# A new opening for the first chunk of a fused attention and expert kernel: row sums by one-column matmuls, the feature map on ScalarE and GpSimd, halves of heads instead of halves of the batch, and other load times

## The chip, the core and the metric

The kernel runs on one core of a Trainium2 chip. A core has TensorE (matmuls and transposes), VectorE, ScalarE and GpSimd for the rest, and SyncE, which here issues nearly all transfers. Each engine works through its own queue in order. The metric is the device time of one execution in microseconds (us). Times inside an execution are counted from its first instruction.

## The reference, cut to what matters

Two batches, eight heads, 576 positions, 64 wide. Attention output is a gated mix of causal softmax attention and of a lookup in a memory matrix through the feature map phi; two feed-forward layers follow.

```python
scores = np.where(causal, -1e9, scale * (q @ k.T))
a = np.exp(scores - scores.max(-1, keepdims=True))
a /= a.sum(-1, keepdims=True) + 1e-09
local = a @ v
phi = lambda x: np.where(x > 0, x, np.exp(x) - 1.0) + 1.0
mem_out = (phi(q) @ M_prev) / ((phi(q) @ z_prev)[..., None] + 1e-06)
x = sigmoid(beta) * mem_out + (1 - sigmoid(beta)) * local   # then to (B*S, H*D)
x = np.maximum(x @ w_in, 0.0) ** 2 @ w_out                  # 512 -> 2048 -> 512
out = sum(p[e] * (np.maximum(x @ w1[e], 0.0) @ w2[e]) for e in range(4))
```

The weights `w_in` and `w_out` reach the chip as float64 words, and the kernel turns them into float32 itself.

## The kernel before, in words

Tokens are cut into nine tiles of 128, in three chunks. Chunk 0 is the first 128 rows of both batches (tiles 7 and 8). Chunk 1 holds rows 128 to 383, chunk 2 the rest. The change touches two stages: the opening, which does the attention of chunk 0, and the stage behind it, in which the first layer of chunk 0 runs on TensorE while the attention of chunk 1 is woven in.

**The opening** (`opening`, called at the end of a block in which every engine keeps the program's order). Its order is a written list of letters. `s0` and `s1` step through the scores of heads 0 to 3 and 4 to 7, each for both batches: first the matmuls (L307), then one maximum per batch (VectorE, L189 and L318), then one exponential per batch (ScalarE, L324), which also gives the row sums by its accumulator. `p0`, `p1` are the halves of the feature map (`phi`, L181 to L184): an exponential on ScalarE, then a minimum and a maximum on VectorE. `m0` to `m2` are the memory matmuls (L405), `n` and `k` their norms and products on VectorE (L410 to L417). `t0` to `t3` transpose the four blocks of exponentials (L336) and copy them out of PSUM, three on VectorE (L339) and one on ScalarE (L341). `v0` to `v3` are the products with the values (L356). `q` turns row sums into weights (L424 to L426), `x0` and `x1` weigh and add one batch each (L432, L433), and `o0`, `o1` transpose the result (L197) and copy it into the layer's input `y` (L438). `g` is the gate, `l` and `L` load the second rows. `c` is a step of the conversion, `S` a step of the first scores of chunk 1, and `w` readies the layer.

**The conversion** (`convert`): each block of 512 KB of float64 words is loaded (L722), read twice by ScalarE (`mag` L734, `bits` L737), joined twice by VectorE (L740, L745), and the float32 block is written back to memory for later chunks (L748). A block's load stands in SyncE's queue behind the write of the block made three blocks before.

**The layer of chunk 0** (`ffn1(0)`) gives one step for each of 128 matmuls of 256 columns: four up (L101) for a block of hidden units, the squared relu (ScalarE L787, VectorE L788), and four down (L802) two blocks later. If a block of weights isn't converted when the layer comes to it, the conversion's steps are put into the queues right there. Before the third up block that holds for the blocks numbered 4 and 5.

**The woven work** (`rest`) has a due step for each item: third rows are loaded (`x.load(2, n)`), the second rows' feature map (`x.phis(1)`, L181 to L184) and memory matmuls (`x.mem(1, ...)`, L365) run, and pairs of heads go through scores, turns, values and blends. A due step is rounded up to a whole step of the layer.

Of the kernel before, what the change touches and what calls it, by code (L numbers as in the profile page):

```python
# [21 lines left out]
P = 128  # L22
# [30 lines left out]
def attention_then_experts(ctx, tc, qa, ka, va, qc, kc, vc, mz, beta, w1, probs, w2, out):  # L53
# [116 lines left out]
    def gates():  # L170
# [5 lines left out]
        nc.vector.tensor_scalar(out=gate1, in0=gate, scalar1=-1.0, scalar2=1.0, op0=ALU.mult, op1=ALU.add)  # L176
        yield

    def phi(out, e, q, hold=lambda x: x):

        hold(nc.scalar.activation(out=e, in_=q, func=AF.Exp))  # L181
        yield
        nc.vector.tensor_scalar_min(e, e, 1.0)
        nc.vector.scalar_tensor_tensor(out=out, in0=q, scalar=1.0, in1=e, op0=ALU.add, op1=ALU.max)  # L184
        yield
# [44 lines left out]
    def opening(c0, c1, first_layer):  # L230

        sc = [c0.scores(p, spot) for p, spot in zip(c0.pairs, (("s", 3), ("pv", 2)))]
        ph, gt, later = c0.phis(0), gates(), c1.scores(c1.pairs[0])
        units = [u for p in c0.pairs for u in p]
        steps = dict(
            g=lambda: next(gt), c=lambda: next(cv), w=lambda: next(first_layer), l=lambda: [c1.load(1, n) for n in range(2)], L=lambda: c1.load(1, 2), S=lambda: next(later, None),
            n=c0.norms, k=c0.recall, q=c0.weights,
        )
        for i in range(2):
            steps[f"s{i}"] = lambda i=i: next(sc[i], None)  # L240
            steps[f"p{i}"] = lambda i=i: next(ph[i])
            steps[f"x{i}"] = lambda i=i: c0.local(i)
            steps[f"o{i}"] = lambda i=i: c0.out(i)
        for i, u in enumerate(units):
            steps[f"t{i}"] = lambda u=u, e=nc.vector if i < 3 else None: c0.turn(u, e)
            steps[f"v{i}"] = lambda u=u: c0.values(u)
        for i in range(3):
            steps[f"m{i}"] = lambda i=i: c0.states(i)


        order = (
            "c l c L s0 p0 p0 g g p1 s1 s0 s0 s0 s1 s1 p1 m0 t0 s1 t2 s0 s1 m1 m2 n t1 v0 v2 k q x0 "
            "t3 c v1 v3 S o0 x1 o1 c S S c w S S S"
        )
        for k in order.split():
            steps[k]()

    def attention_a(c, pool, eng, banks):
# [25 lines left out]

        def phis(r):
            e = q[r][1] = pool.tile([P, H, P], F32, tag="phia", name="phia", bufs=2)
            return [phi(e[:, hs], e[:, hs], q[r][0][:, hs]) for hs in (slice(0, 4), slice(4, 8))]

        def s_(pair, spot=None):
            scs = {}  # L290
            tag, bufs = spot or ("s", banks[1])
            for u in pair:
                t, kn, h0, nh = u
                b = TILES[t][0][0]
                if h0 + b == 0:
                    sms[t] = pool.tile([P, B, H], F32, tag="sm", name="sm", bufs=2)
                if h0 == 0:
                    st[t] = [pool.tile([P, H], F32, tag=x, name=x, bufs=4) for x in ("mx", "nb")] + [sms[t - b][:, b]]
# [45 lines left out]
        def v_(u):  # L344
            t, kn, h0, nh = u
            b = TILES[t][0][0]
            at = at_.pop(u)
# [47 lines left out]
            b = TILES[t][0][0]  # L395
            finish(t, xls[t - b][:, b], banks[0], banks[2])()

        pms, fs = [], [pool.tile([P, B, H], F32, name=f"f{i}", bufs=1) for i in range(2 * (c == 0))]
        third = (slice(0, 3), slice(3, 6), slice(6, 8))

        def states(i):
            ps, tag, bufs = (banks[0], "m", banks[2]) if i < 2 else (ps_h, "h", 1)
            pms.append(ps.tile([P, 3, B, D + 1], F32, tag=tag, name="pm", bufs=bufs))
            for k, h in enumerate(range(third[i].start, third[i].stop)):
                nc.tensor.matmul(pms[i][:, k], lhsT=q[0][1][:, h, :], rhs=mzd[:, h], start=True, stop=True)  # L405

        def norms():
            for pm, hs in zip(pms, third):
                n = hs.stop - hs.start
                nc.vector.tensor_scalar_add(fs[1][:, :, hs], pm[:, 0:n, :, D].rearrange("p h b -> p b h"), 1e-6)  # L410
            nc.vector.reciprocal(out=fs[1], in_=fs[1])
            nc.vector.tensor_mul(fs[1], fs[1], gate[:, None, :].to_broadcast([P, B, H]))

        def recall():
            for pm, hs in zip(pms, third):
                n = hs.stop - hs.start
                nc.vector.tensor_mul(  # L417
                    q[0][2][:, :, hs, 0:D].rearrange("p b h d -> p h b d"), pm[:, 0:n, :, 0:D],
                    fs[1][:, :, hs].rearrange("p b h -> p h b")[:, :, :, None].to_broadcast([P, n, B, D]),
                )  # L420

        def weights():
            for b in range(B):
                nc.vector.tensor_scalar_add(fs[0][:, b], st[CHUNKS[0][0] + b][2], 1e-9)  # L424
            nc.vector.reciprocal(out=fs[0], in_=fs[0])
            nc.vector.tensor_mul(fs[0], fs[0], gate1[:, None, :].to_broadcast([P, B, H]))  # L426

        def local(b):
            xl = xls[b] = pool.tile([P, H, D], F32, tag="xl0", name="xl0", bufs=2)
            for i in range(2):  # L430
                hs = slice(4 * i, 4 * i + 4)
                nc.vector.tensor_mul(xl[:, hs], pvs[CHUNKS[0][0], i][:, b], fs[0][:, b, hs, None].to_broadcast([P, 4, D]))  # L432
            nc.vector.tensor_add(xl, xl, q[0][2][:, b, :, 0:D])  # L433

        def out_(b):
            tp = banks[0].tile([P, NK, P], F32, tag="m", name="tp", bufs=banks[2])
            upright(tp, xls[b])
            nc.scalar.activation(out=first_x[:, :, b * P:b * P + P], in_=tp, func=AF.Copy)  # L438

        return SimpleNamespace(  # L440
            pairs=pairs, load=load, load_v=load_v, phis=phis, scores=s_, turn=t_, values=v_, mem=mem, recalled=recalled, weigh=weigh, blend=blend, stand=stand,
            states=states, norms=norms, recall=recall, weights=weights, local=local, out=out_,
        )

    def value_scale(pool, banks):
# [24 lines left out]
    def rest(x, scale, cv):  # L470
# [21 lines left out]
        for i, pair in enumerate(x.pairs):  # L492
# [750 lines left out]
```

## Time and profile before

| | |
|---|---|
| median of 3 runs | 689.8 us (689.16 to 690.34) |
| profiled execution, its own time | 696.75 us |
| span from first to last instruction | 694.6 us |
| TensorE busy | 669.6 us, 96% of the span |
| VectorE, ScalarE, GpSimd busy | 513.4, 442.6, 141.6 us |
| mean granted TensorE clock | 0.993 of full speed |

The profiled execution is a single one and took 1% longer than the median. Busy shares are means over stages with different limits, so a stage has to be read by itself. In a timeline a line may stand for several instructions; the bracket at its end gives the idle time of the engine ahead of it and what ended it.

### The profile page before, as it was taken

How to read it: one execution, taken by the hardware profiler on the slowest of the kernel's cores; microseconds unless marked ns; L12 is line 12 of the kernel's file. 1: busy time of each engine (PE TensorE's matmuls, PEld its weight loads, DVE VectorE, ACT ScalarE, POOL GpSimd, SP SyncE). 2: the span in 40 equal slices, each digit the busy share in tenths (PEclk: the TensorE clock that was granted, in tenths of full speed). 3: DMA queues.
4: the chain of work that ended last, by engine and by line, in shares of the span. 5: the costliest groups of instructions: out<-in, count | busy, mean ns of one | idle time of the engine just before them, and what ended most of it. 6: DMA issues, size and time to landing. Idle time of an engine off the chain costs nothing. (4 is left out here: it accounts for less than half of the span.)

```text
span 694.6 us, 12446 instructions
## 1 busy us (share of the span) xinstructions
PE 669.6 (96%) x4604; PEld 483.6 (70%) x4604; DVE 513.4 (74%) x1011; ACT 442.6 (64%) x830; POOL 141.6 (20%) x197
## 2 busy tenths in 40 slices
PE   7799999899999999999999999999999999999997
PEld 4588878677877879999766666656655555555553
DVE  7879787599996586779689679787765856665743
ACT  5689976798686448966888677545534435353430
POOL 1010010000000022004335443433332242423200
PEclk9999999999999999999999999999999999999999
DMA  8798875679955636965122332333341323000002
GB/s 292 259 345 299 283 264 171 210 210 254 259 130 129 120 86 215 328 213 156 62 91 92 122 122 69 127 110 122 107 136 62 103 81 96 25 1 1 1 1 76
DMA packets 65565, 101.24 MB, mean 146 GB/s; under 512 B 32673, under 2 KB 34977, under 8 KB 65505
## 3 DMA queue, kind: packets, MB, share of 16 engines
q1 hardware_dynamic: 65216, 100.32, 47.2%
q8 instruction: 36, 0.59, 0.3%
q14 instruction: 25, 0.20, 0.1%
q10 hardware_dynamic: 288, 0.14, 0.1%
HBM read 82.87 MB, written 10.75 MB: 135 GB/s over the span
## 5 line engine op out<-in xcount | busy, mean ns | idle before, releaser
L1115 PE MATMUL o<-w,g 128*128 128x512 f16 x864 | 216.9, 379 | 0.0
L1017 PE MATMUL pe<-xs,wu 128*128 128x256 f16 (+1 forms) x1344 | 196.2, 286 | 3.1 <-DVE u L1039 2.3
L1017 PEld LDWEIGHTS <-wu 128*128 128x128 f16 x1344 | 130.8, 98 | 72.1 <-issue 6.2
L1115 PEld LDWEIGHTS <-g 128*128 128x128 f16 x864 | 84.5, 98 | 67.7 <-issue 0.2
L1033 ACT ACTIVATE g<-h 128x512 f16<-128x512 f32 (+1 forms) x64 | 43.4, 678 | 106.8 <-DVE h L1039 100.6
L804 PE MATMUL y<-g,w 128*128 128x512 f32 (+1 forms) x384 | 88.9, 369 | 0.7 <-DVE w L84 0.7
L983 POOL TENSOR_TENSOR ws<-raw 128x256 f32<-128x256 f32 x32 | 24.6, 769 | 259.1 <-DVE wu L980 132.9
L804 PEld LDWEIGHTS y<-g,w 128*128 128x128 f32 x384 | 68.2, 188 | 8.0 <-DVE w L84 1.0
L1034 DVE SCALAR_TENSOR_TENSOR g<-h,g 128x512 f16<-128x512 f32 (+1 forms) x64 | 51.6, 806 | 23.3 <-ACT g L1033 23.0
L1039 DVE SCALAR_TENSOR_TENSOR u<-pe,p 128x256 f32<-128x256 f32 (+1 forms) x64 | 28.8, 451 | 37.4 <-PE pe L1017 35.9
L106 PE MATMUL hpb<-x,w 128*128 128x512 f32 x192 | 53.0, 411 | 1.2 <-DVE r L788 1.2
L84 DVE TENSOR_TENSOR w<-wraw,w 128x512 fp32r<-128x512 f32 x64 | 45.3, 715 | 10.5 <-ACT w L83 10.4
L1039 DVE SCALAR_TENSOR_TENSOR h<-pe,u 128x256 f32<-128x256 f32 (+1 forms) x64 | 29.0, 453 | 29.9 <-PE pe L1017 29.6
L83 ACT ACTIVATE w<-wraw 128x512 fp32r<-128x512 f32 x64 | 39.6, 625 | 17.7 <-PE y L804 10.5
L980 DVE SCALAR_TENSOR_TENSOR wu<-ws,wpow,wu 128x512 f16<-128x512 f32 x64 | 45.6, 750 | 1.9 <-ACT wu L991 1.9
L189 DVE CUSTOM_DVE_ANT_0 a<-sc,mask 128x384 f32<-128x384 f32 (+4 forms) x80 | 36.5, 479 | 14.1 <-PE sc L589 9.9
L925 DVE SCALAR_TENSOR_TENSOR w<-raw,wpow,w 128x1024 f16<-128x1024 f32 x32 | 41.4, 1294 | 1.8 <-ACT w L924 1.3
L106 PEld LDWEIGHTS hpb<-x,w 128*128 128x128 f32 x192 | 35.5, 193 | 9.8 <-DVE r L788 2.4
L991 ACT ACTIVATE wu<-ws,wpow 128x1024 f16<-128x1024 f32 x32 | 36.4, 1137 | 6.4 <-POOL ws L988 6.4
L985 ACT ACTIVATE wu<-raw,wpow 128x768 f16<-128x768 f32 x32 | 29.8, 932 | 13.4 <-PE pe L1017 11.5
L980 DVE SCALAR_TENSOR_TENSOR wu<-raw,wpow,wu 128x768 f16<-128x768 f32 x32 | 33.2, 1039 | 6.1 <-ACT wu L985 5.7
L924 ACT ACTIVATE w<-raw,wpow 128x1024 f16<-128x1024 f32 x32 | 36.3, 1134 | 0.0
(172 smaller groups left out, 1101.9 us busy)
## 6 DMA issues: line engine op xcount, KB each, us to landing
raw<-in_w SPq DMA_DIRECT2D x64, 512.0 KB, 3.7
w<-in_w SPq DMA_DIRECT2D x32, 512.0 KB, 5.4
wraw<-w1s SPq DMA_DIRECT2D x64, 256.0 KB, 3.2
w1s<-bits SPq DMA_DIRECT2D x32, 256.0 KB, 3.7
kraw<-in_kc SPq DMA_DIRECT2D x8, 576.0 KB, 4.8
vraw<-in_vc SPq DMA_DIRECT2D x8, 320.0 KB, 3.7
qraw<-in_qc SPq DMA_DIRECT2D x4, 512.0 KB, 4.6
out<-acc SPq DMA_DIRECT2D x7, 256.0 KB, 2.0
```

The costliest lines, as they stand in the source:

```text
L83: nc.scalar.activation(out=w[:, 0], in_=raw, func=AF.Copy)
L84: eng.tensor_sub(w[:, 1], raw, w[:, 0].bitcast(F32))
L106: nc.tensor.matmul(acc, lhsT=w[:, a, kk * P:(kk + 1) * P], rhs=xs_r[c][:, b, kk, :], start=(i == 0), stop=(i == 3 * NK - 1),)
L189: nc.vector.tensor_tensor_reduce(out=dst, in0=sc, in1=msk, op0=ALU.add, op1=ALU.max, scale=1.0, scalar=-3.0e38, accum_out=m)
L804: nc.tensor.matmul(yacc[d], lhsT=w[:, a, d * P:(d + 1) * P], rhs=g[:, b], start=(first and i == 0), stop=(last and i == 2),)
L925: nc.vector.scalar_tensor_tensor(out=w1, in0=x, scalar=s, in1=w0, op0=ALU.mult, op1=ALU.subtract)
L980: nc.vector.scalar_tensor_tensor(out=w[:, 1, ks], in0=x, scalar=s1, in1=w[:, 0, ks], op0=ALU.mult, op1=ALU.subtract)
L1017: nc.tensor.matmul(acc, lhsT=w[:, wa, k, kk * P:kk * P + P], rhs=x[:, xb, kk], start=(m == 0 and not onto), stop=(m == 5), skip_group_chec ...
L1033: nc.scalar.activation(out=g[:, 0], in_=hm, func=AF.Relu)
L1034: nc.vector.scalar_tensor_tensor(out=g[:, 1], in0=hm, scalar=0.0, in1=g[:, 0], op0=ALU.max, op1=ALU.subtract)
L1039: nc.vector.scalar_tensor_tensor(out=out, in0=acc, scalar=HID, in1=x, op0=ALU.mult, op1=ALU.add)
L1115: nc.tensor.matmul(outs[t], lhsT=gs[i, m][:, gb, r:r + P], rhs=wds[i, m][:, wa], start=(p == 0 and m == 0 and wa == gb), stop=(p == 3 and ...
```

## The change

The opening is rearranged. The exponentials of chunk 0 no longer accumulate row sums: `sums(i)` makes them on TensorE, one matmul for each head with the turned exponentials as weights and one column of ones, into the free end of the first memory tile's PSUM room. The feature map of the first rows becomes `phi_first`: three ScalarE activations and an addition on GpSimd. All four turns are copied by ScalarE. Weights and products go by halves of heads over both batches (`weights(i)`, `local(i)`), the memory part is added by batch (`join(b)`: batch 0 on VectorE, batch 1 on GpSimd). The written order is new. In the woven stage the third rows are loaded later, the second rows' feature map comes sooner, and a few due steps of scores, turns, blends and memory matmuls move by less than two steps.

```diff
+    def phi_first(out, r, q, eng):
+        nc.scalar.activation(out=out, in_=q, func=AF.Relu, scale=-1.0)
+        nc.scalar.activation(out=out, in_=out, func=AF.Exp, scale=-1.0)
+        nc.scalar.activation(out=r, in_=q, func=AF.Relu)
+        yield
+        eng.tensor_add(out, out, r)
+        yield
...
-            steps[f"t{i}"] = lambda u=u, e=nc.vector if i < 3 else None: c0.turn(u, e)
+            steps[f"t{i}"] = lambda u=u: c0.turn(u)
...
-            "c l c L s0 p0 p0 g g p1 s1 s0 s0 s0 s1 s1 p1 m0 t0 s1 t2 s0 s1 m1 m2 n t1 v0 v2 k q x0 "
-            "t3 c v1 v3 S o0 x1 o1 c S S c w S S S"
+            "g g c s0 l c L p0 p1 p0 s1 s0 s0 s0 s1 s0 s1 m0 t0 p1 s1 m1 m2 n t1 s1 "
+            "v0 t2 v1 z0 q0 k x0 t3 c v2 v3 z1 q1 x1 y1 S y0 S c w o0 o1 S S c S S"
...
-                        accum_out=sm[:, h0 + i:h0 + i + 1],
+                        accum_out=sm[:, h0 + i:h0 + i + 1] if c else None,
...
+        def sums(i):
+            for u in pairs[i]:
+                at, b = at_.pop(u), TILES[u[0]][0][0]
+                for h in range(4):
+                    nc.tensor.matmul(
+                        sms[CHUNKS[0][0]][:, b, 4 * i + h:4 * i + h + 1], lhsT=at[:, h * P:h * P + P], rhs=ones[:, 0:1],
+                        start=True, stop=True,
+                    )
...
+        def weights(i):
+            hs = slice(4 * i, 4 * i + 4)
+            cf = cfs[i] = pool.tile([P, B, 4], F32, tag="cg", name="cg", bufs=2)
+            nc.vector.tensor_scalar_add(cf, sms[CHUNKS[0][0]][:, :, hs], 1e-9)
+            nc.vector.reciprocal(out=cf, in_=cf)
+            nc.vector.tensor_mul(cf, cf, gate1[:, None, hs].to_broadcast([P, B, 4]))
+
+        def local(i):
+            if i == 0:
+                xls[0] = pool.tile([P, B, H, D], F32, tag="xl", name="xl", bufs=2)
+            nc.vector.tensor_mul(
+                xls[0][:, :, 4 * i:4 * i + 4], pvs[CHUNKS[0][0], i], cfs[i][:, :, :, None].to_broadcast([P, B, 4, D])
+            )
+
+        def join(b):
+            (nc.gpsimd if b else nc.vector).tensor_add(xls[0][:, b], xls[0][:, b], q[0][2][:, b, :, 0:D])
...
-        for n, m in enumerate((5.66, 11.7, 13.7)):
+        for n, m in enumerate((18.0, 21.65, 32.3)):
             plan(m, lambda n=n: x.load(2, n))
-        for r, ps_, ms in ((1, (6.17, 9.23), (12.59, 16.15, 20.15)), (2, (41.21, 51.06), (63.46, 67.46, 72.53))):
+        for r, ps_, ms in ((1, (3.75, 6.81), (13.39, 16.95, 20.95)), (2, (41.21, 51.06), (64.16, 67.46, 72.53))):
...
-                for d in (5.18, 0.29, 3.11, 5.2) if last else (0.04, 0.14, 0.78, 0.85):
+                for d in (3.71, 0.29, 3.11, 5.72) if last else (0.04, 0.14, 0.69, 0.87):
...
-            for u, d in zip(pair, (10.84, 11.84) if last else (0.4, 0.6)):
+            for u, d in zip(pair, (10.84, 11.84) if last else (0.42, 0.6)):
...
-                plan(m + 2.5, lambda t=t, h=h0 // 4: x.blend(t, h))
+                plan(m + 2.0, lambda t=t, h=h0 // 4: x.blend(t, h))
...
-                    plan(m + (5 if last else 7.5) + 4.0 * n, lambda t=u[0]: x.stand(t))
+                    plan(m + (5.5 if last else 8.0) + 4.0 * n, lambda t=u[0]: x.stand(t))
...
-            plan(30.0 + 7 * n, lambda: next(scale))
+            plan(29.5 + 7 * n, lambda: next(scale))
```

## Rows read from the trace of the kernel before

**Rows 1.** The page's first part: busy time, share of the span, instructions.

```profile
PE 669.6 (96%) x4604; PEld 483.6 (70%) x4604; DVE 513.4 (74%) x1011; ACT 442.6 (64%) x830; POOL 141.6 (20%) x197
```

**Rows 2.** The timeline, TensorE: start, us, line, operation, count, idle ahead.

```profile
21.72 1.99 PE L101 MATMUL hpa<-y,bits 128*128 128x256 f32 x8 [0.74 <-ACT y L438]
...
28.09 0.70 PE L101 MATMUL hpa<-y,bits 128*128 128x256 f32 x2 [1.36 <-DVE g L788]
...
30.80 1.46 PE L802 MATMUL y<-g,bits 128*128 128x256 f32 x6
35.33 0.94 PE L365 MATMUL pm<-mzd,phia 128*128 128x130 f32 x6 [3.07 <-DVE phia L184]
...
36.63 1.98 PE L356 MATMUL pv<-va,at 128*64 128x64 f32 x32
...
40.31 1.56 PE L101 MATMUL hpa<-y,bits 128*128 128x256 f32 x6
```

**Rows 3.** Windows: stretch, length, busy of five engines, clock, DMA share, GB/s.

```profile
36.00:37.00 1.00, 1.00 (x11) 0.67 (x11) 1.00 (x3) 1.00 (x5) 0.00 (x0) 0.79 1.05 416
37.00:38.00 1.00, 1.00 (x26) 1.00 (x24) 0.97 (x2) 1.00 (x4) 0.00 (x0) 0.50 1.04 397
...
39.00:40.00 1.00, 1.00 (x14) 1.00 (x14) 0.00 (x0) 1.00 (x4) 0.00 (x0) 0.50 1.06 406
```

**Rows 4.** The timeline, ScalarE and SyncE's queue, 23 to 33 us.

```profile
23.73 0.33 SPq L765 DMA_DIRECT2D wraw<-w1s  x1
...
24.97 0.38 SPq L722 DMA_DIRECT2D w<-in_w  x1
...
31.56 0.66 ACT L734 ACTIVATE mag<-w 128x512 f32<-128x512 f32 x1 [2.93 <-DMA w<-in_w]
...
32.67 0.61 ACT L181 ACTIVATE phia<-qa 128x512 f32<-128x512 f32 x1
```

**Rows 5.** The timeline, ScalarE, 8 to 22 us.

```profile
8.21 0.63 ACT L181 ACTIVATE phia<-qa 128x512 f32<-128x512 f32 x1 [2.65 <-DMA qa<-in_qa]
...
8.74 0.38 ACT L324 ACTIVATE a<-a,nb 128x128 f32<-128x128 f32 x1
...
9.04 0.18 ACT L324 ACTIVATION_READ_ACCUMULATOR a<-a,nb 128x1 f32 x1
...
20.58 1.09 ACT L438 ACTIVATE y<-tp 128x512 f32<-128x512 f32 x2 [2.81 <-PE tp L197]
```

**Rows 6.** Groups by line and form: count, busy us, mean ns of one.

```profile
L356 PE MATMUL pv<-va,at 128*64 128x64 f32 x384 | 15.3, 234 | 3.0 <-DVE xl L432 1.7 <-ACT at L341 1.3
...
L405 PE MATMUL pm<-mzd,phia 128*128 128x130 f32 x16 | 2.3, 286 | 0.4 <-DMA mzd<-in_mz 0.4
```

**Rows 7.** The timeline, VectorE: what the later steps of the opening cost.

```profile
15.15 1.34 DVE L417 TENSOR_TENSOR xm<-pm,f 128x384 f32<-128x384 f32 x3
...
20.03 0.68 DVE L740 SCALAR_TENSOR_TENSOR bits<-mag,bits 128x512 int32<-128x512 int32 x1
...
21.35 0.42 DVE L189 CUSTOM_DVE_ANT_0 a<-sc,mask 128x256 f32<-128x256 f32 x1
...
22.24 0.42 DVE L189 CUSTOM_DVE_ANT_0 a<-sc,mask 128x256 f32<-128x256 f32 x1
...
46.24 0.17 DVE L382 TENSOR_SCALAR cg<-sm 128x8 f32<-128x8 f32 x1
...
52.66 0.68 DVE L391 TENSOR_TENSOR xl<-pv,cg 128x512 f32<-128x512 f32 x1
```

**Rows 8.** The timeline, GpSimd and VectorE side by side, 48 to 51 us.

```profile
48.21 2.49 POOL L377 TENSOR_TENSOR xm<-xm,cf 128x512 f32<-128x512 f32 x2 [43.99 <-DVE cf L375]
...
48.49 1.30 DVE L740 SCALAR_TENSOR_TENSOR bits<-mag,bits 128x512 int32<-128x512 int32 x1 [0.47 <-ACT bits L737]
...
49.96 0.42 DVE L189 CUSTOM_DVE_ANT_0 a<-sc,mask 128x256 f32<-128x256 f32 x1 [0.17 <-PE sc L307]
```

**Rows 9.** The word blocks' loads up to 60 us: issue to landing.

```profile
DMA to landing us min/median/max: 3.7/6.0/8.2
```

More of the change, by code (lines that the diff above doesn't have):

```diff
@@ L236, in opening @@
             g=lambda: next(gt), c=lambda: next(cv), w=lambda: next(first_layer), l=lambda: [c1.load(1, n) for n in range(2)], L=lambda: c1.load(1, 2), S=lambda: next(later, None),
-            n=c0.norms, k=c0.recall, q=c0.weights,
+            n=c0.norms, k=c0.recall,
         )
@@ L241, in opening @@
             steps[f"p{i}"] = lambda i=i: next(ph[i])
+            steps[f"q{i}"] = lambda i=i: c0.weights(i)
+            steps[f"z{i}"] = lambda i=i: c0.sums(i)
             steps[f"x{i}"] = lambda i=i: c0.local(i)
+            steps[f"y{i}"] = lambda i=i: c0.join(i)
             steps[f"o{i}"] = lambda i=i: c0.out(i)
         for i, u in enumerate(units):
-            steps[f"t{i}"] = lambda u=u, e=nc.vector if i < 3 else None: c0.turn(u, e)
+            steps[f"t{i}"] = lambda u=u: c0.turn(u)
             steps[f"v{i}"] = lambda u=u: c0.values(u)
@@ L286, in phis @@
             e = q[r][1] = pool.tile([P, H, P], F32, tag="phia", name="phia", bufs=2)
-            return [phi(e[:, hs], e[:, hs], q[r][0][:, hs]) for hs in (slice(0, 4), slice(4, 8))]
+            halves = slice(0, 4), slice(4, 8)
+            if r == 0:
+                p = pool.tile([P, H, P], F32, name="phip", bufs=1)
+                return [phi_first(e[:, hs], p[:, hs], q[r][0][:, hs], eng) for hs, eng in zip(halves, (nc.gpsimd, nc.gpsimd))]
+            return [phi(e[:, hs], e[:, hs], q[r][0][:, hs]) for hs in halves]
         def s_(pair, spot=None):
@@ L294, in s_ @@
                 b = TILES[t][0][0]
-                if h0 + b == 0:
+                if h0 + b == 0 and c:
                     sms[t] = pool.tile([P, B, H], F32, tag="sm", name="sm", bufs=2)
                 if h0 == 0:
-                    st[t] = [pool.tile([P, H], F32, tag=x, name=x, bufs=4) for x in ("mx", "nb")] + [sms[t - b][:, b]]
+                    st[t] = [pool.tile([P, H], F32, tag=x, name=x, bufs=4) for x in ("mx", "nb")] + [sms[t - b][:, b] if c else None]
                 scs[u] = banks[0].tile([P, 512], F32, tag=tag, name="sc", bufs=bufs)
@@ L346, in v_ @@
             b = TILES[t][0][0]
-            at = at_.pop(u)
+            at = at_.pop(u) if c else at_[u]
             half = t - b, h0 // 4
@@ L396, in stand @@
             finish(t, xls[t - b][:, b], banks[0], banks[2])()
-        pms, fs = [], [pool.tile([P, B, H], F32, name=f"f{i}", bufs=1) for i in range(2 * (c == 0))]
+        pms, fn = [], pool.tile([P, B, H], F32, name="fn", bufs=1) if c == 0 else None
         third = (slice(0, 3), slice(3, 6), slice(6, 8))
@@ L402, in states @@
             ps, tag, bufs = (banks[0], "m", banks[2]) if i < 2 else (ps_h, "h", 1)
-            pms.append(ps.tile([P, 3, B, D + 1], F32, tag=tag, name="pm", bufs=bufs))
+            room = ps.tile([P, 512], F32, tag=tag, name="pm", bufs=bufs)
+            pms.append(room[:, 0:3 * B * (D + 1)].rearrange("p (h b d) -> p h b d", h=3, b=B))
+            if i == 0:
+                sms[CHUNKS[0][0]] = room[:, 512 - B * H:].rearrange("p (b h) -> p b h", b=B)
             for k, h in enumerate(range(third[i].start, third[i].stop)):
                 nc.tensor.matmul(pms[i][:, k], lhsT=q[0][1][:, h, :], rhs=mzd[:, h], start=True, stop=True)
+        def sums(i):
[6 more added lines that the diff above has]
+                    )
         def norms():
@@ L409, in norms @@
                 n = hs.stop - hs.start
-                nc.vector.tensor_scalar_add(fs[1][:, :, hs], pm[:, 0:n, :, D].rearrange("p h b -> p b h"), 1e-6)
-            nc.vector.reciprocal(out=fs[1], in_=fs[1])
-            nc.vector.tensor_mul(fs[1], fs[1], gate[:, None, :].to_broadcast([P, B, H]))
+                nc.vector.tensor_scalar_add(fn[:, :, hs], pm[:, 0:n, :, D].rearrange("p h b -> p b h"), 1e-6)
+            nc.vector.reciprocal(out=fn, in_=fn)
+            nc.vector.tensor_mul(fn, fn, gate[:, None, :].to_broadcast([P, B, H]))
         def recall():
@@ L418, in recall @@
                     q[0][2][:, :, hs, 0:D].rearrange("p b h d -> p h b d"), pm[:, 0:n, :, 0:D],
-                    fs[1][:, :, hs].rearrange("p b h -> p h b")[:, :, :, None].to_broadcast([P, n, B, D]),
+                    fn[:, :, hs].rearrange("p b h -> p h b")[:, :, :, None].to_broadcast([P, n, B, D]),
                 )
[L422 to L433, printed above, removed]
+        def weights(i):
[5 more added lines that the diff above has]
+        def local(i):
+            if i == 0:
+                xls[0] = pool.tile([P, B, H, D], F32, tag="xl", name="xl", bufs=2)
[4 more added lines that the diff above has]
+            (nc.gpsimd if b else nc.vector).tensor_add(xls[0][:, b], xls[0][:, b], q[0][2][:, b, :, 0:D])
         def out_(b):
             tp = banks[0].tile([P, NK, P], F32, tag="m", name="tp", bufs=banks[2])
-            upright(tp, xls[b])
+            upright(tp, xls[0][:, b])
             nc.scalar.activation(out=first_x[:, :, b * P:b * P + P], in_=tp, func=AF.Copy)
@@ L441, in attention_a @@
             pairs=pairs, load=load, load_v=load_v, phis=phis, scores=s_, turn=t_, values=v_, mem=mem, recalled=recalled, weigh=weigh, blend=blend, stand=stand,
-            states=states, norms=norms, recall=recall, weights=weights, local=local, out=out_,
+            states=states, sums=sums, norms=norms, recall=recall, weights=weights, local=local, join=join, out=out_,
         )
```

## The prediction

> **What bounds the kernel now.** The page's first part comes first: TensorE is busy 96% of the span [rows 1], so an edit pays where it removes a wait of TensorE, or a stretch at a low clock, and costs where it makes one. The timeline of TensorE shows where such waits are near the change. In the opening TensorE mostly waits, up to the layer's first matmul at 21.72; whatever delays that matmul delays everything behind it. After it TensorE idles twice: 1.36 us until 28.09, for the squared relu that frees a PSUM tile, and 3.07 us until 35.33, for the second rows' feature map [rows 2]. The windows show a consequence: 1 us after the long wait ended, the granted clock falls from full speed to half, 0.79 in the microsecond from 36, then 0.50 in the three up to 40 [rows 3]. That is 0.21 + 3 x 0.5 = 1.7 us of TensorE's work. The timeline of ScalarE and of SyncE's queue says what was late: word block 5, whose load was issued at 24.97, reached ScalarE at 31.56 after 2.93 us of waiting, and the feature map stood behind it in ScalarE's queue, at 32.67 [rows 4]. So the common end point to compare is 40.31, where TensorE has done the first down block, one memory matmul group, the first values and the next scores. From there to the chunk's end both kernels give TensorE the same work.
>
> **The opening.** Its start stays: SyncE's order of loads is unchanged, and the second half of the queries lands at 8.21 [rows 5]. From there ScalarE sets the pace. A relu must be complete before the exponential behind it reads it, 0.65; the exponential and the second relu take 0.55 each, as two such reads filled 31.56 to 32.67 [rows 4]. That gives 9.95, where before the exponentials of the scores began at 8.74. One of these took 0.30 up to its accumulator read, and the read goes away [rows 5]: eight take 2.4, to 12.35. A copy of a turn takes 0.50 with the next behind it (two in 1.09) [rows 5], then four exponentials 1.2, then the second copy to its end 0.6: 14.65.
>
> TensorE then does the values of the second batch, 16 instructions at 15.3/384 = 0.04, to 15.3, and the new sums: 8 matmuls, 16 instructions. No row has one column. From below they are priced by the 64-column values, 0.04 each, 0.64 a step; from above by the 130-column memory matmuls, 2.3/16 = 0.144, 2.3 a step [rows 6]. With one column only the weight load is left, and it has twice the columns of the values' load, so I take 0.08, or 1.28, nearest to the lower row. First sums: 16.6. The Trainium skill, page "TensorE: Matmul & The Clock Gate", section "LDWEIGHTS (loading the stationary operand)", prices a load by its columns alone, at 107 ns for 128 of them; by that a step is 1.7 us and the estimate for the opening 0.85 us longer. It would give 53 ns for 64 columns, where the row here has 40 for load and matmul together, so I stay with the row.
>
> VectorE's order now puts the weights ahead of the recall, so both wait for the sums, though the recall could start earlier. Weights: three small ones at 0.17, 0.52; recall 1.34; product 0.68 [rows 7]: 19.1. Meanwhile TensorE turns the last block (0.6), ScalarE copies it (0.6), then values 0.64 and second sums 1.28, to 19.75. Behind these on VectorE: weights 0.52, product 0.68, the join 0.69 like its form at 20.03, to 21.65; a maximum of chunk 1, 22.24 - 21.35 = 0.89; and the join of word block 0, 21.35 - 20.03 = 1.32 [rows 7]. That is 23.85, without contention. Removed from VectorE are the second feature map half, three copies and one of the additions, but they bring nothing here, since VectorE then waits for the sums.
>
> GpSimd adds the other batch at the same time. One such operation takes 2.49/2 = 1.25, done near 22.2, and its turn and copy are ready before 23.85. But while GpSimd ran, a VectorE operation with two tensors from SBUF took 1.30, not 0.68; a maximum, which reads PSUM, kept its 0.42 [rows 8]. So the feature map's additions on GpSimd, under maxima, cost nothing, and the join on VectorE costs between 0 and 0.6; I take 0.3, since it starts first. The Trainium skill, "GPSIMD Engine Reference", section "1. Specifications", says that the two engines share SBUF interfaces and contend when VectorE has two SBUF inputs; its rule would put the full 0.6 here, and 0.3 on the sum. The two rows just read bear it out for the word blocks.
>
> So the layer starts at 24.2, **2.5 us later** than 21.72. Bounds: cheap sums without contention 2.5 - 1.3 - 0.3 = 0.9 later, dear sums with contention 2.5 + 2.0 + 0.3 = 4.8 later.
>
> **The woven stage.** TensorE needs 28.09 - 21.72 - 1.36 = 5.0 for two up blocks and the scores between, to 29.2. VectorE joins word blocks 0 and 1 back to back now. Behind them come a maximum 0.89, ScalarE's two exponentials of a unit and a block's reads, about 2.1, the relu on both engines 0.8: a wait of about 0.6 is left of the 1.36, to 29.8. From there to the first down block 30.80 - 28.09 = 2.7, and four matmuls 2.0: 34.5 [rows 2].
>
> The feature map's first half now is due at step 4, ahead of the forced block 5, so the memory matmuls find it ready and the 3.07 goes. What is late next is block 5 itself. Its load stands behind the write of block 1, joined at 24.2 + 1.3 = 25.5, and goes out 0.4 later, at 25.9. Landing took 3.7 to 8.2, median 6.0 [rows 9], and 6.6 for this block before: I take 6.0, to 31.9. Behind it ScalarE has this block's reads 1.1, a turn's copy 0.5, the second feature map half 0.55, the next block's reads 1.1 and the second turn's copy 0.6, to 35.75. The values need that copy, so TensorE waits 1.25 there instead of 3.07 elsewhere. Values and scores took 40.31 - 36.63 = 3.7, of which the clock took 1.7, so 2.0; the memory matmuls take 0.9 [rows 2, 3]. End: 38.7 against 40.31, **1.6 us earlier**. In terms: -0.75 and -1.8 of waits, -1.7 of clock, +2.5 of opening, which leaves -1.7.
>
> The third rows' loads were issued after block 5's and didn't delay it; moved, they have at least 16 steps of 0.5 until the scores that read them, and woven work between, so they cost nothing, unless they land at their slowest. Each of their six issues stands in SyncE's queue ahead of a word load there, where three blocks lie ahead. The other due steps round up to the same step or the next one. I price them at nothing; TensorE's queue of ready work covers one step, 0.5 us.
>
> The sum is made on the profiled execution, 694.6 us of span plus 2.15 around it, 696.75; the median of the runs is 689.8, 7 us lower, and I carry the difference over: 689.8 - 1.6 = **688.2 us**. Its own range follows block 5: landing after 3.7, no wait, 2.9 earlier; after 6.6, 1.0 earlier: 686.9 to 688.8. About 0.2% (1.4 us) is what can be told from no change.
>
> **Rivals.**
> *The opening is cheap.* Sums at 0.04 and no contention bring the layer 1.6 earlier than in my sum, 3.2 in all, 686.6. For it: the lower row is the same kind of matmul. Against it: full-width weights.
> *The gain is used up in the opening.* Either sums at 0.144 each, +2.0 to 690.2, or the clock: TensorE idles near 21 and again near 23, a good 1 us each, around matmuls of one column. If that halves the clock for as long as before, 1.7 goes: 689.9. Against the clock: 1.36 us of idle alone was not followed by a fall [rows 2].
> *Word block 5 starves the stage; slower.* The word loads sit still until block 0 is joined, which is 2.5 later. SyncE's queue also holds a read-back of block 0's write (23.73 [rows 4]), which waits some 2.2 us for that write to land. Before, it fell into a gap; if it again stands ahead of block 1's write, block 5 goes out near 27.3, lands after 6.6 at 33.9, and TensorE waits for the values until 37.75. A wait of 3.2 like the old one brings the fall of the clock: 37.75 + 2.9 + 1.7 = 42.4, 2.1 later, 691.9. It decides from a landing near 33.5 on.
>
> **Chances.** Forecast 0.38, cheap opening 0.16, gain used up 0.24, starved 0.22. Two thirds of the forecast's range and the cheap opening are faster by over 0.2%, with a little of the third: 0.45. The rest of the forecast and most of the used-up case make 0.33 within 0.2%, and 0.22 are slower. The range reaches from the cheap opening with block 5 early, 686.0, to most of the starved case, 691.4.
>
> **What would show it.** Right: a layer start between 23 and 25; ScalarE busy without a gap from 8.2 to 16; VectorE idle ahead of the first weights; the memory matmuls without a wait; full clock from 30 to 45; a wait near 1 us ahead of the values. Wrong: sums far from 1.3 a step, a half clock anywhere between 20 and 40, or block 5 reaching ScalarE after 33.5.

## The result: 0.55% slower, where 0.2% faster was forecast

The changed kernel takes 693.68 us (median of 8 runs, 692.27 to 696.33), the kernel before 689.97 (8 runs, 688.93 to 691.45): a ratio of 1.0055, 95% interval 1.0038 to 1.0072, so **3.7 us slower**. The forecast was 688.2 with a range of 686.0 to 691.4. The time lies outside it.

A line number belongs to the kernel whose rows it stands in; in the changed kernel the sums are L430. The changed kernel's timeline of TensorE (start, us, line, operation, count, idle ahead):

```profile
15.34 1.95 PE L430 MATMUL pm<-ones,at 128*128 128x1 f32 x16
...
17.71 1.72 PE L372 MATMUL pv<-va,at 128*64 128x64 f32 x32
19.36 3.58 PE L430 MATMUL pm<-ones,at 128*128 128x1 f32 x16
22.86 2.08 PE L323 MATMUL sc<-ka,qa 64*128 64x128 f32 x16
25.08 2.15 PE L206 MATMUL tp<-ident,xl 128*128 128x128 f32 x8
27.92 3.78 PE L101 MATMUL hpa<-y,bits 128*128 128x256 f32 x8 [0.69 <-ACT y L470]
31.63 1.49 PE L323 MATMUL sc<-ka,qa 64*128 64x128 f32 x16
...
39.64 1.15 PE L372 MATMUL pv<-va,at 128*64 128x64 f32 x32
...
42.69 1.56 PE L101 MATMUL hpa<-y,bits 128*128 128x256 f32 x6
```

Set it beside [rows 2]. The two waits of 1.36 and 3.07 us are gone. But the layer starts at 27.92 instead of 21.72, and the common end point, the next up block behind the scores, comes at 42.69 instead of 40.31. In front of the layer stand the two steps of one-column sums (L430). The first takes 1.95 us, the second, the same 16 instructions, 3.58. The page's first part says "busy" to all of this:

```profile
PE 677.4 (98%) x4636; PEld 490.5 (71%) x4636; DVE 509.9 (73%) x1003; ACT 445.3 (64%) x821; POOL 145.3 (21%) x200
```

TensorE is busier than before, 677.4 us against 669.6 [rows 1]; that is no gain, since part of it is the new sums and part the same work at a lower clock. The windows show the clock (columns as in [rows 3]: behind the busy times of the five engines stand the granted clock, the DMA share and GB/s):

```profile
12.00:18.00 6.00, 6.00 (x81) 5.37 (x81) 1.50 (x10) 4.07 (x12) 0.00 (x0) 1.00 1.05 400
18.00:20.00 2.00, 1.93 (x33) 1.67 (x30) 1.78 (x4) 2.00 (x4) 0.00 (x0) 0.67 0.81 213
20.00:24.00 4.00, 4.00 (x24) 3.98 (x26) 0.93 (x4) 0.64 (x2) 0.00 (x0) 0.50 0.04 12
24.00:28.00 4.00, 3.17 (x19) 2.15 (x16) 3.90 (x10) 1.32 (x3) 1.69 (x1) 0.50 0.00 0
28.00:32.00 4.00, 4.00 (x10) 2.81 (x12) 2.95 (x9) 4.00 (x13) 0.00 (x0) 0.50 0.91 278
32.00:36.00 4.00, 3.93 (x30) 3.15 (x29) 2.81 (x11) 2.87 (x8) 0.00 (x0) 0.96 0.80 313
```

From the stretch 18 to 20 on the clock falls, and from 20 to 32 it stands at 0.50, the lower level of 1.2 GHz. TensorE had not waited at all in the six microseconds before. (From about 8.5 to 11.9 the clock stood at half as well; ScalarE, which sets the pace there, shows no wait for it.) The DMA share of 0.04 and 0.00 shows the other side of the delay: the word loads stand still until the first blocks are joined.

VectorE's timeline shows who waits for the sums:

```profile
17.32 0.17 DVE L453 TENSOR_SCALAR cg<-pm 128x8 f32<-128x8 f32 x1 [3.47 <-PE pm L430]
...
22.97 0.17 DVE L453 TENSOR_SCALAR cg<-pm 128x8 f32<-128x8 f32 x1 [3.19 <-PE pm L430]
...
24.34 0.69 DVE L465 TENSOR_TENSOR xl<-xl,xm 128x512 f32<-128x512 f32 x1
```

Both steps of sums are on the path: VectorE stands idle 3.47 and 3.19 us until they end.

**How executions are compared below.** The second half of the queries lands at another time in each execution. So an end point is counted from the start of ScalarE's second feature map half, which reads them; it is called T here. In the changed kernel ScalarE works from T to 15.96 without a wait, so the count fits it: 42.69 - 7.84 = 34.85, where the forecast was 38.7 - 8.21 = 30.5. For the kernel before it gives 40.31 - 8.21 = 32.10 [rows 2, 5], and for a second profile of that kernel (run e8, below) 38.94 - 6.81 = 32.13. That these two agree is chance. In e8 the layer starts 1.06 later from T, and the long wait is 1.03 shorter. VectorE, not T, paces the old opening: in both profiles its maxima begin at 7.07 or 7.08, and it waits at most 0.24 us from there to the layer, which starts at 21.72 and 21.38. So for the kernel before the count is good to about 1 us. Counted from the first instruction, the changed kernel's end point is 2.4 us behind the first profile of before and 3.75 behind the second.

### The profile page after: what moved, and what is told of

Its sections match the earlier page's. It is cut to its first block, busy times and chain, and to the rows that moved or that the text cites. A ratio compares the mean times of both kernels' runs of the same rounds, so it can differ in the third digit from the quotient of the medians.

```text
span 694.2 us, 12493 instructions
## 1 busy us (share of the span) xinstructions
PE 677.4 (98%) x4636; PEld 490.5 (71%) x4636; DVE 509.9 (73%) x1003; ACT 445.3 (64%) x821; POOL 145.3 (21%) x200
## 5 line engine op out<-in xcount | busy, mean ns | idle before, releaser
L101 PE MATMUL hpa<-y,bits 128*128 128x256 f32 x128 | 35.9, 403 | 0.8 <-ACT y L470 0.7
```

## The experiments

| run | median us | ratio to before, 95% | layer from T | end point from T |
|---|---|---|---|---|
| before (two profiles) | see below the table | 1 | 13.51, 14.57 | 32.10, 32.13 |
| after | 693.68 | 1.0055 (1.0038, 1.0072) | 20.08 | 34.85 |
| e1, new opening without the sums | 688.50 | 0.9960 (0.9943, 0.9976) | 14.68 | 28.63 |
| e2, old opening with the sums | 697.05 | 1.0076 (1.0053, 1.0099) | 21.63 | 37.02 |
| e3, new due steps alone | 689.33 | 0.9972 (0.9958, 0.9985) | 15.01 | 30.30 |
| e4, new opening alone | 694.35 | 1.0042 (1.0026, 1.0059) | 17.99 | 33.85 |
| e5, after with filled sums | 693.77 | 1.0038 (1.0022, 1.0055) | 20.19 | 33.27 |
| e6, e1 with old due steps | 689.27 | 0.9975 (0.9956, 0.9993) | 14.69 | 29.27 |
| e7, e1 with shared copies | 688.06 | 0.9951 (0.9933, 0.9969) | 14.50 | 28.75 |
| e9, after with halved sums | 689.84 | 0.9988 (0.9970, 1.0007) | 15.37 | 29.63 |
| e10, exponentials first | 689.42 | 0.9988 (0.9972, 1.0004) | | |
| e11, e10 and recall first | 690.18 | 1.0003 (0.9987, 1.0020) | | |

The kernel before ran beside them: 691.38 us (26 runs, for e1 to e4), 691.13 (28, e5 to e8) and 690.76 (29, e9 to e11). In e10 and e11 the second feature map half itself is moved, so T means nothing there. Each profile is a single execution. In the window from 8 to 12 its granted clock is 0.51 to 0.58 in after, e1, e2, e3, e5, e10 and e11 and 1.00 in the other six; in e3 and e5 the half clock lasts to about 15, so their layer column holds some of that. Like stands beside like in e1 and after, and in e6 and e4.

### e1: the change without its sums

The accumulators come back, all else of the change stays.

```diff
-            "v0 t2 v1 z0 q0 k x0 t3 c v2 v3 z1 q1 x1 y1 S y0 S c w o0 o1 S S c S S"
+            "v0 t2 v1 q0 k x0 t3 c v2 v3 q1 x1 y1 S y0 S c w o0 o1 S S c S S"
...
-                        accum_out=sm[:, h0 + i:h0 + i + 1] if c else None,
+                        accum_out=sm[:, h0 + i:h0 + i + 1],
```

> The changed kernel with the row sums back in the exponentials' accumulator and the sixteen one-column matmuls left out, everything else kept. If the sums cost the time (5.5 us of TensorE in the opening and a clock at half speed from 18.8 to 32.2 us), the clock stays full there, the layer starts near 23 to 24 us instead of 27.9, and the time is 687 to 690 us. If the opening is slow because ScalarE paces it, with the sums only filling a wait, the layer still starts after 26 us and the time stays at 692 us or above.

688.50 us, 0.9960 of before. Against the changed kernel that is 0.95% by the ratios, 6.6 us (5.2 by the medians; before ran at 691.38 beside e1 and at 689.97 beside the changed kernel). TensorE's timeline:

```profile
22.57 1.97 PE L101 MATMUL hpa<-y,bits 128*128 128x256 f32 x8 [0.78 <-DVE bits L775]
...
27.86 0.70 PE L101 MATMUL hpa<-y,bits 128*128 128x256 f32 x2 [0.19 <-DVE g L818]
...
33.94 0.69 PE L372 MATMUL pv<-va,at 128*64 128x64 f32 x16 [0.86 <-ACT at L357]
...
36.52 1.56 PE L101 MATMUL hpa<-y,bits 128*128 128x256 f32 x6
```

The layer starts 5.35 us earlier, its first up block takes 1.97 instead of 3.78, and all windows from 12 to 40 show the full clock. The mean granted clock of each run agrees: 0.995 to 0.998 in e1's nine, 0.987 to 0.993 in the eight of the changed kernel. The rest of the change is a gain.

### e2: the sums alone, in the old opening

```diff
-            "c l c L s0 p0 p0 g g p1 s1 s0 s0 s0 s1 s1 p1 m0 t0 s1 t2 s0 s1 m1 m2 n t1 v0 v2 k q x0 "
-            "t3 c v1 v3 S o0 x1 o1 c S S c w S S S"
+            "c l c L s0 p0 p0 g g p1 s1 s0 s0 s0 s1 s1 p1 m0 t0 s1 t2 s0 s1 m1 m2 n t1 v0 v2 z0 k "
+            "t3 z1 q x0 c v1 v3 S o0 x1 o1 c S S c w S S S"
...
-                        accum_out=sm[:, h0 + i:h0 + i + 1],
+                        accum_out=sm[:, h0 + i:h0 + i + 1] if c else None,
```

> The kernel before with nothing changed but the sums: one-column matmuls ahead of the weights instead of the accumulator, in the old order. If the sums are the cause, TensorE spends about 2 us on each of the two steps at full clock or more, the layer starts 2 to 5 us later than before, and the time is 2 to 5 us above the kernel before. If they only matter in the new order, the time is within 1 us of the kernel before.

697.05 us, 1.0076: the worst of all. TensorE's timeline, and under it the windows:

```profile
15.48 1.95 PE L415 MATMUL pm<-ones,at 128*128 128x1 f32 x16
...
18.07 3.41 PE L415 MATMUL pm<-ones,at 128*128 128x1 f32 x16 [0.16 <-DVE xm L430]
...
29.27 1.99 PE L101 MATMUL hpa<-y,bits 128*128 128x256 f32 x8 [0.69 <-ACT y L450]
```

```profile
16.00:20.00 4.00, 3.84 (x27) 3.61 (x27) 1.35 (x3) 1.70 (x3) 0.00 (x0) 0.79 0.81 257
20.00:24.00 4.00, 2.78 (x31) 2.70 (x33) 2.17 (x7) 0.00 (x0) 0.00 (x0) 0.50 0.01 2
24.00:28.00 4.00, 4.00 (x37) 3.66 (x34) 3.47 (x10) 0.23 (x1) 0.00 (x0) 0.50 0.00 0
```

The same two prices, 1.95 and 3.41, and the same fall of the clock: it comes with the sums, whatever opening stands around them. The layer starts 7 to 8 us later from T than before, more than expected; in this order all sums stand ahead of the weights of both halves. Whether the sums cost more here than in the changed kernel isn't shown: the two intervals overlap, and e2 lacks what the rest of the change gains.

### e3 and e4: the new due steps alone, the new opening alone

e3 is the kernel before with the diff's lines of due steps; e4 is the changed kernel with the old ones:

```diff
-        for n, m in enumerate((18.0, 21.65, 32.3)):
+        for n, m in enumerate((5.66, 11.7, 13.7)):
...
-        for r, ps_, ms in ((1, (3.75, 6.81), (13.39, 16.95, 20.95)), (2, (41.21, 51.06), (64.16, 67.46, 72.53))):
+        for r, ps_, ms in ((1, (6.17, 9.23), (12.59, 16.15, 20.15)), (2, (41.21, 51.06), (63.46, 67.46, 72.53))):
```

> The kernel before with the new due steps of the woven stage alone (third rows later, second rows' feature map sooner, small moves). If the prediction's account of the waits holds, the 3.07 us wait ahead of the memory matmuls goes, and the time is 0 to 3 us below the kernel before. If the new due steps are what makes the changed kernel slow, it is 2 to 4 us above.

> The changed kernel with the old due steps in the woven stage: the new opening alone. If the opening is the cause, the time is at least as far above the kernel before as the change as a whole, 3 to 7 us. If the due steps are the cause, it is within 1.5 us of the kernel before.

e3 gains, 0.9972; e4 loses, 1.0042, by an interval that overlaps that of the whole change. In e3 the memory matmuls no longer wait, and TensorE waits at the values instead, as forecast (the wait of 1.36 for the squared relu stays):

```profile
36.13 0.69 PE L356 MATMUL pv<-va,at 128*64 128x64 f32 x16 [1.14 <-ACT at L341]
...
38.70 1.56 PE L101 MATMUL hpa<-y,bits 128*128 128x256 f32 x6
```

In the profile of e4 both steps of sums ran at the full clock, 1.95 each. The clock falls only behind them:

```profile
13.97 1.95 PE L430 MATMUL pm<-ones,at 128*128 128x1 f32 x16
...
17.72 1.95 PE L430 MATMUL pm<-ones,at 128*128 128x1 f32 x16
...
24.66 3.78 PE L101 MATMUL hpa<-y,bits 128*128 128x256 f32 x8 [0.69 <-ACT y L470]
```

The layer comes 17.99 after T, 3.3 later than in e6 (below), which differs by the sums alone. These 3.3 hold the transposes at half clock, 2.16 for eight, and the up block takes 3.78.

### e5: matmuls put between the sums, to keep the clock

```diff
                 for h in range(4):
                     nc.tensor.matmul(
...
+                for _ in range(2):
+                    nc.tensor.matmul(fill, lhsT=wt[:, 0:P], rhs=wt, start=True, stop=True)
```

> The changed kernel with two 512-column bf16 matmuls into an unread PSUM tile after each batch's sums, eight in all: 1.7 us more work for TensorE in the opening at full clock, none of it useful. If the half clock behind the sums comes from the low activity of one-column matmuls, the clock stays at full speed through 18 to 32 us and the kernel is no slower, or faster by up to 4 us, than the changed kernel in spite of the added work (690 to 694 us). If the sums cost only the time they take, the time rises by 1.5 to 2 us, to 695 us or above.

693.77 us, 1.0038 of before; the changed kernel is at 1.0055, and the intervals overlap. TensorE's timeline and one window:

```profile
17.41 1.05 PE L431 MATMUL pm<-ones,at 128*128 128x1 f32 x8
18.32 0.38 PE L436 MATMUL fill<-wt 128*128 128x512 bf16 x1
...
28.80 1.97 PE L101 MATMUL hpa<-y,bits 128*128 128x256 f32 x8 [0.78 <-ACT y L473]
```

```profile
24.00:28.00 4.00, 3.01 (x28) 1.95 (x27) 3.57 (x12) 0.60 (x1) 1.69 (x1) 1.00 0.00 0
```

Every window from 16 to 40 has the full clock, and the first up block takes 1.97. That isn't one lucky profile: the mean granted clock is 0.994 to 0.998 in all twelve runs of e5, 0.987 to 0.993 in all eight of the changed kernel, 0.993 to 1.000 in the 28 of the kernel before beside e5. Eight wide matmuls that nobody reads cost no more than they save. So the fall of the clock is a price of its own, apart from the length of the sums, and more work among them kept the clock up.

### e6 and e7: the rest of the opening, and the best kernel

e6 is e1 with the old due steps. e7 is e1 with two of the four turns copied by VectorE again:

```diff
-            steps[f"t{i}"] = lambda u=u: c0.turn(u)
+            steps[f"t{i}"] = lambda u=u, e=nc.vector if i in (0, 2) else None: c0.turn(u, e)
```

> The new opening without the sums and with the old due steps. With sums and due steps as the only two parts that matter, this is within 1 us of the kernel before. If the rest of the new opening (feature map on ScalarE and GpSimd, copies on ScalarE, halves of heads) costs, as the prediction's account of ScalarE says, it is 1 to 2 us above; if it gains, 1 to 2 us below.

> The new opening without the sums, new due steps, and the first and third turn copied by VectorE instead of ScalarE. If ScalarE sets the pace of the opening, as the prediction had it, the layer starts up to 1 us sooner than with all copies on ScalarE (22.6 us) and the time is 0 to 1 us below the 688.5 us of that kernel. If VectorE's later steps set it, nothing changes or it is slower by up to 1 us.

e6 gives 0.9975: without the sums the new opening gains by itself. Its layer starts no sooner from T than before's (14.69 against 13.51 and 14.57), but the wait of 1.36 for the squared relu is 0.18 there, since word blocks 0 and 1 are joined back to back. The wait ahead of the memory matmuls is 1.67, where the kernel before had 3.07 and 2.04, and no fall of the clock follows it. e7 is the best kernel of all, 688.06 us, **0.9951 (0.9933 to 0.9969)**, below both the kernel before and the changed one; its interval overlaps that of e1, so the shared copies themselves are not shown to gain. Its timeline and windows hold something else:

```profile
22.20 3.34 PE L101 MATMUL hpa<-y,bits 128*128 128x256 f32 x8 [0.78 <-DVE bits L775]
...
36.45 1.56 PE L101 MATMUL hpa<-y,bits 128*128 128x256 f32 x6
```

```profile
20.00:24.00 4.00, 2.83 (x13) 2.06 (x12) 3.90 (x12) 3.15 (x8) 0.70 (x1) 0.83 0.32 91
24.00:28.00 4.00, 4.00 (x26) 2.96 (x24) 2.56 (x11) 2.85 (x9) 0.00 (x0) 0.75 0.97 337
```

Here the clock falls without any sums, behind waits of 0.7, 0.4 and 0.8 us, where e1 with nearly the same waits (0.4, 0.4, 0.8) kept it.

### e8: the kernel before, profiled once more

> The kernel before once more, for a second profile of it. Its first profiled execution took 696.75 us where its runs have a median near 690 to 691. If the 1.98 us wait ahead of the second late transpose near 122 us and the half clock behind it belong to the kernel, they show again; if they are an accident of that execution, the profile has no wait there and a span near 688 to 690 us.

Its own time is 690.16 us. TensorE's timeline:

```profile
21.38 1.99 PE L101 MATMUL hpa<-y,bits 128*128 128x256 f32 x8 [0.74 <-ACT y L438]
...
27.75 0.70 PE L101 MATMUL hpa<-y,bits 128*128 128x256 f32 x2 [1.36 <-DVE g L788]
...
33.95 0.94 PE L365 MATMUL pm<-mzd,phia 128*128 128x130 f32 x6 [2.04 <-DVE phia L184]
...
38.94 1.56 PE L101 MATMUL hpa<-y,bits 128*128 128x256 f32 x6
...
120.14 0.60 PE L197 MATMUL tp<-ident,xl 128*128 128x128 f32 x4
```

Both waits are there, and the fall of the clock (0.87 and 0.70 in the windows 32 to 36 and 36 to 40). The long wait is 2.04 instead of 3.07, so its size isn't fixed. The wait near 122 us of the first profile is gone, and with it the half clock behind it (1.00 in the windows from 120 to 128); that was an accident of the first execution:

```profile
123.97 0.66 PE L197 MATMUL tp<-ident,xl 128*128 128x128 f32 x4 [1.98 <-DVE x L206]
```

ScalarE's timeline of e8 shows T, and that the exponentials behind it wait for VectorE's maxima:

```profile
6.81 0.63 ACT L181 ACTIVATE phia<-qa 128x512 f32<-128x512 f32 x1 [1.25 <-DMA qa<-in_qa]
8.24 0.40 ACT L324 ACTIVATE a<-a,nb 128x128 f32<-128x128 f32 x1 [0.80 <-DVE nb L318]
```

### e9: the sums as pairs of 64 weight columns

```diff
-                    nc.tensor.matmul(
-                        sms[CHUNKS[0][0]][:, b, 4 * i + h:4 * i + h + 1], lhsT=at[:, h * P:h * P + P], rhs=ones[:, 0:1],
-                        start=True, stop=True,
-                    )
+                    for p in range(0, P, 64):
+                        nc.tensor.matmul(
+                            sms[CHUNKS[0][0]][p:p + 64, b, 4 * i + h:4 * i + h + 1], lhsT=at[:, h * P + p:h * P + p + 64],
+                            rhs=ones[:, 0:1], start=True, stop=True,
+                        )
```

> The changed kernel with each one-column sum split into two of 64 weight columns, side by side in the array like the values: twice the instructions, the same sums. If the price of a sum is its weight load by columns, and the values' row of 0.04 us for such a pair holds with one column, a step takes 1.3 us at full clock instead of 1.95, and the time is 1 to 2 us below the changed kernel (692 to 693 us). If each instruction has a fixed price of about 0.12 us, a step takes 3.9 us and the time is 3 us or more above the changed kernel.

689.84 us, 0.9988: the loss goes, 0.67% or 4.6 us by the ratios to before, more than expected. TensorE's timeline:

```profile
14.17 1.05 PE L431 MATMUL pm<-ones,at 128*64 128x1 f32 x32
...
17.01 1.05 PE L431 MATMUL pm<-ones,at 128*64 128x1 f32 x32
...
22.69 3.61 PE L101 MATMUL hpa<-y,bits 128*128 128x256 f32 x8 [0.78 <-ACT y L471]
```

Twice as many instructions take 1.05 instead of 1.95: 0.033 each, not half of 0.122. The Trainium skill, page "TensorEngine Tiling (Array Packing)", section "Tiling Modes", says that different parts of the array can load weights and multiply at the same time; these rows agree. The loads of the sums show it too: a half-width one takes 138 ns on average and one comes every 33, a full-width one 191 and one comes every 122. No run has half-width loads that stay in one half, so how much the alternation does is not shown. The second step isn't slowed here, but the clock falls later, over the first up block (0.83 and 0.75 in the windows 20 to 24 and 24 to 28). At the full clock two steps cost 1.8 us less; that the rest of the 4.6 is the clock's fits its mean, 0.991 to 1.000 in the runs of e9 and 0.987 to 0.993 in those of the changed kernel.

### e10 and e11: two tries to get further

e10 puts the first batch's exponentials ahead of the second feature map half in e7; e11 also puts the recall ahead of the weights:

```diff
-            "g g c s0 l c L p0 p1 p0 s1 s0 s0 s0 s1 s0 s1 m0 t0 p1 s1 m1 m2 n t1 s1 "
+            "g g c s0 l c L p0 s0 s0 s0 s1 p1 p0 s1 s0 s1 m0 t0 p1 s1 m1 m2 n t1 s1 "
...
-            "v0 t2 v1 q0 k x0 t3 c v2 v3 q1 x1 y1 S y0 S c w o0 o1 S S c S S"
+            "v0 t2 v1 k q0 x0 t3 c v2 v3 q1 x1 y1 S y0 S c w o0 o1 S S c S S"
```

> The new opening without the sums, with two turns copied by VectorE, and the first batch's exponentials put ahead of the second feature map half, where ScalarE waits for queries. If ScalarE's work after the queries' landing sets the opening, as the prediction had it, 1.2 us of it moves into that wait and the layer starts 0.5 to 1.2 us sooner after the landing than the 14.4 us without this: 687 to 688 us. If VectorE's later steps set it, the time stays at 688 us.

> The same with the recall put ahead of the first weights on VectorE, where it stood behind them. If VectorE waits there for weights, 1.3 us of its work moves into the wait and the layer starts up to 1 us sooner than without: 686.5 to 687.5 us. If the weights are ready by then, nothing changes.

Both miss: 0.9988 and 1.0003, where e7 had 0.9951. In e10 ScalarE waits 1.48 us for the maxima and starts the exponentials only at 8.18; the second feature map half slides to 9.74, and a memory matmul group waits 0.87 for it at 12.93. The layer starts at 23.40, in e11 at 23.52, against 22.20 in e7; both profiles were at half clock up to about 11.7, that of e7 was not. In the opening the feature map belongs first, since the maxima need the time that it fills.

## Why the prediction was wrong

The direction was wrong, and the step that failed is one term of the sum: **the one-column sums, taken at 0.08 us an instruction and 1.28 a step, with TensorE at its full clock**. Both halves of it failed. The amount can be followed to the end point, which came 34.85 - 30.5 = 4.35 us later than forecast, counted from T.

*Up to VectorE's second weights.* Forecast 19.75 - 8.21 = 11.54 from T, measured 22.97 - 7.84 = 15.13: 3.6 later. Each step of sums took 1.95 at the full clock, 0.67 over the 1.28, so 1.34 for two. The clock added 3.58 - 1.95 = 1.63 to the second. The first began 0.4 later than forecast, and between the two went another 0.2.

*From there to the layer.* Forecast 24.2 - 19.75 = 4.45, measured 27.92 - 22.97 = 4.95: 0.5 later. The layer now waited for the copy of the turned result, whose transposes ran at half clock (2.15 for eight; 1.09 in e3).

*From the layer to the end point.* Forecast 38.7 - 24.2 = 14.5, measured 14.77, but by another way. Half clock cost 3.78 - 1.97 on the first up block and 1.49 - 1.16 on the scores, 2.14. In return TensorE was so slow that the two waits of 0.6 and 1.25 didn't come, 1.85. Together 3.6 + 0.5 + 0.3 = 4.4.

Of that, the load of the weights took 1.34, and the clock 1.63 + 0.5 + 0.3 = 2.4, if the 0.5 is counted as its own. e1 takes the whole term away and is 0.95% faster than the changed kernel, e2 adds it to the kernel before and is 0.76% slower than that, e9 makes it cheaper and is 0.67% faster than the changed kernel: the cause is shown from three sides. The split between load and clock is read from one profile; e5 shows that the clock has a share.

**Why 0.08 was wrong.** The row that it leant on, the 64-column values at 0.04, is not a cheaper load of the same kind: the loop at the values alternates between the two column halves, as e9 does, and such loads overlap (one every 0.033 in e9). Full-width instructions follow each other every 0.122. The Trainium skill, page "TensorE: Matmul & The Clock Gate", section "LDWEIGHTS (loading the stationary operand)", gave 107 ns, or 1.7 a step; measured were 1.95, and the rule that the prediction set aside was nearer than its row. The upper bound of 2.3, from the 130-column row, held at the full clock; the second step, at half clock, went over it.

**Why the clock was missed.** The prediction looked for a fall only around TensorE's waits, priced it at 1.7 us "for as long as before", and set it as an alternative to dear sums. The profile after shows full clock from 12 to 18, no wait in the six microseconds ahead, and then half clock through to 32. The rival "the gain is used up in the opening" was the right place, but both of its causes came together, and the half clock lasted four times as long as before (some 13 us against 3.5). The loss that this rival named was 0.4 us at most, 690.2; it became 3.7.

**The other steps:**

- *ScalarE's chain* held: the second turn's copy ends at 14.31, 6.47 from T, forecast 6.44. The timeline of ScalarE after shows T, the exponentials without accumulator from 9.56 on, 1.72 from T (forecast 1.74), eight in 2.43, as priced (0.30 each), and the copy:

```profile
7.84 0.63 ACT L181 ACTIVATE phia<-qa 128x512 f32<-128x512 f32 x1 [0.89 <-DMA qa<-in_qa]
...
9.56 2.43 ACT L340 ACTIVATE a<-a,nb 128x128 f32<-128x128 f32 x8
...
13.73 0.58 ACT L357 ACTIVATE at<-atp 128x512 f32<-128x512 f32 x1
```

- *The feature map's addition on GpSimd* costs nothing, as forecast; *the join* was priced at 0.3 more on VectorE, and there it cost nothing (0.69 above). A price of that size fell on the other engine: 1.69 instead of 1.27. In e5 and e9, at full clock there, TensorE waits 0.39 us for it ahead of the second transposes, and the layer waits for the copy behind them. GpSimd's timeline:

```profile
9.73 1.27 POOL L185 TENSOR_TENSOR phia<-phia,phip 128x512 f32<-128x512 f32 x1 [1.36 <-ACT phip L183]
24.38 1.69 POOL L465 TENSOR_TENSOR xl<-xl,xm 128x512 f32<-128x512 f32 x1 [13.38 <-DVE xl L460]
```

- *The woven stage* held in its mechanism. The memory wait is gone, TensorE waits at the values instead (1.25 forecast; 0.86 in e1, 1.14 in e3, none in e5), and the due steps alone gain (e3). In the changed kernel the half clock hides this.
- *The opening besides the sums* was forecast as no gain, since VectorE would wait for the sums. Without these it gains 0.25% (e6). What shrank clearly in the profiles is the wait for the squared relu: 0.6 was to be left of it, 0.18 (e6) and 0.19 (e1) were.
- *Moved loads of the third rows* cost nothing: up to 130 us TensorE waits for no load but the first queries.
- *Word block 5 starves the stage*, the rival on the slower side, didn't occur. The read-back was issued at 36.54, behind the loads that it could have delayed, and no wait at the values came.
- *The base* of the sum was one execution, at 696.75 us. In e8 the wait ahead of the memory matmuls, of which the sum took 1.8 us away, was 2.04 and not 3.07, and the old layer start didn't follow the queries' landing. So the gain forecast there was about 1 us too large for an execution like e8. That is the smaller error, and of the same sign: 4.35 and 1.0 are about the 5.3 by which the medians missed the forecast difference, though single profiles scatter as much. The median in this comparison, 689.97, is 0.2 above the 689.8 used.

**What stays open.** At the end point the changed kernel is 2.4 to 3.75 us behind before in the profiles, by its median 3.7. The other kernels with the new opening come out up to 1.6 us slower than the count from T says (e6 -2.9 by the end point, -1.9 by the median; e9 -2.5 and -0.9). It isn't found in one profile of each: from the end point to the last instruction, two profiles of the kernel before differ by 654.3 - 649.1 = 5.2 us. And why the clock falls in one profile behind short waits (e7, e9) and not in another (e1, e6), or at about 8 us in some profiles only, isn't settled by these runs.

## What to carry to other kernels

Price a matmul with few columns by its weight load, from a row of the same weight width and the same change of column halves, and split it into two halves of the columns where the output allows: 32 half-width instructions took 1.05 us, 16 full-width ones 1.95. A TensorE that is busy without a wait can still lose its clock, as here behind thin matmuls (few columns for each weight load): put them on the path only with the price of the clock behind them added, for all that TensorE does until the clock is back. Read the granted clock of every run, not of one profile alone: the clock of a single profile differed between like kernels, the runs' means told them apart. And before you count a stage from an event, check that its chain starts there: for the old opening it didn't, and two profiles agreed to 0.03 us by chance, their layer starts 1.06 apart.

## What the runs showed of the hardware

- Thin matmuls let the granted clock fall though TensorE doesn't wait: in the changed kernel, 6.00 of 6.00 us busy at 1.00, then 12 us at 0.50. Eight 512-column matmuls among the sums kept it at 1.00 (e5, and the mean clock of its twelve runs).
- One full-width fp32 weight load with a one-column matmul takes 0.122 us at the full clock, a half-width one in alternating column halves 0.033.
- When GpSimd and VectorE work on two SBUF tensors at the same time, either can pay: VectorE's join of a word block took 1.30 instead of 0.68 in [rows 8], and here GpSimd's addition took 1.69 instead of 1.27, while VectorE kept 0.69. In both the one that began later paid (VectorE at 48.49 behind GpSimd at 48.21; GpSimd at 24.38 behind VectorE at 24.34). The Trainium skill, "GPSIMD Engine Reference", section "1. Specifications", names this contention; no run has that GpSimd addition without VectorE beside it, so the 1.27 is that of its other addition of the same form.
- The second half of the queries let ScalarE begin between 6.8 and 8.6 us in the profiles in which it waited for them, 6.8 and 8.2 of them for one and the same kernel.
